# Loading two heads of keys and of values with one DMA in a cached-attention decode kernel

## The chip, the cores and the metric

The kernel runs on one core of one Trainium2 chip (trn2). The metric is device time in microseconds (us) of one execution. A trace shows one of these executions; its span, from the first to the last recorded work of the core, is about 2 us shorter than the time.

## The reference

One token passes through attention over the last 4096 positions of a key and value cache with 32 heads of 128 (64 MiB in bfloat16), and through a small gated MLP whose output multiplies the attention's.

```python
# W = 4096, 32 heads, Dh = 128, D = 512
q = (xn @ wq) per head
scores = q . k[:, last W positions] * Dh**-0.5
o = softmax(scores) @ v[:, last W positions]
s = o.reshape(1, 1, 32 * 128) @ wo
g = silu(B(xn))            # layer norms, w1..w4, gelu; at S = 1 its shifted terms are zero
out = x + s * g
```

## The kernel before

Every load goes through one queue, issued by the SyncE engine (SP) in program order, and the transfers finish in that order. One load brings one head: 128 partitions, 8 KiB in each (32 consecutive positions), 1 MiB.

```python
G = 4;  LAG = 5;  K_BUFS = 12;  V_BUFS = 7

def load(dst, src):
    return tc.keep_in_program_order(nc.sync.dma_start(out=dst, in_=src))
...
def load_kv(pool, cache, h):
    t = pool.tile([P, NC, Dh], BF16, tag="kv", name="kv")
    load(t[:], cache[0, h, W0:, :].rearrange("(p c) d -> p c d", p=P))
    return t
```

Even key heads go to VectorE (a product with the broadcast query, `prod`, then a sum, `sS`). Odd key heads go to TensorE: 32 transposes into `pt`, copied by ScalarE to `kt`, then 32 products `sT`. After four heads (a group) the softmax is formed on VectorE and TensorE. Values follow five heads behind the keys: 32 products per head into `oT`, then `o`. Heads are projected with `wo` in blocks of eight after a `repack` of `o`; the last heads with single rows of `wo` (`wo_rows`, `wo_few`).

```python
for i in range(H + LAG):
    if i < H:
        k_head(i, load_kv(k_pool, A_k_cache, i))
    ...
    if i >= LAG:
        h = i - LAG
        if h == H - 1:
            load_rows(h_part, H - G - h_part)      # wo rows of heads 26, 27
        v = load_kv(v_pool, A_v_cache, h)
        if h in (7, 15, 23):
            load_wo((h + 1) // 8 - 1)              # takes a buffer of the key ring
        ...
        if h == H - 1:
            load_rows(H - G, G - 1)
            load_rows(H - 1, 1)
        v_head(h, v)
```

The order within each engine is chosen when the program is built, not only by this text: a different set of loads can give a different order.

Of the kernel before, what the change touches and what calls it, by code (L numbers as in the profile page):

```python
# [8 lines left out]
P = 128  # L9
BF16 = mybir.dt.bfloat16  # L10
# [7 lines left out]

G = 4
LAG = 5  # L20
K_BUFS = 12
NE = 4
V_BUFS = 7


@with_exitstack
def kernel(
# [14 lines left out]
    nc = tc.nc  # L42

    Bb, Sq, D = A_x.shape
    assert Bb == 1 and Sq == 1, "decode kernel: B == Sq == 1"
    _, H, Sk, Dh = A_k_cache.shape
# [3 lines left out]
    W0 = Sk - W  # L50
    assert W == 4096
    NC = W // P
# [6 lines left out]

    k_pool = ctx.enter_context(tc.tile_pool(name="k", bufs=K_BUFS))  # L60
    kt_pool = ctx.enter_context(tc.tile_pool(name="kt", bufs=2))
# [13 lines left out]
    def load(dst, src):  # L75
        return tc.keep_in_program_order(nc.sync.dma_start(out=dst, in_=src))  # L76
# [14 lines left out]
    wq_sb = wts.tile([P, KC, HD], BF16, name="wq_sb")  # L91
    load(wq_sb[:], A_wq.rearrange("(p c) n -> p c n", p=P))

    def load_kv(pool, cache, h):
        t = pool.tile([P, NC, Dh], BF16, tag="kv", name="kv")
        load(t[:], cache[0, h, W0:, :].rearrange("(p c) d -> p c d", p=P))
        return t

    ident_bf = const.tile([P, P], BF16, name="ident_bf")
# [143 lines left out]
    for c in range(2):  # L243
        nc.vector.tensor_copy(
            out=few[:, c, 0:4 * NE].rearrange("p (a b) -> p a b", b=4),
# [14 lines left out]
    def flush():  # L260
        while pending:
            qk(*pending.pop(0))

    def k_head(h, kn):
        g, hl = divmod(h, G)
        if hl == 0:
            st[g] = {
                "sT": ps_s.tile([P, G // 2, NC], FP32, tag="sT", name="sT"),
                "sS": sm_pool.tile([P, G // 2, NC], FP32, tag="sS", name="sS"),
            }  # L270
        s = st[g]
        if h % 2 == 0:
            prod = prod_pool.tile([P, NC, Dh], BF16, tag="prod", name="prod")
            nc.vector.tensor_tensor(out=prod[:], in0=kn[:],  # L274
                                    in1=q_bc[:, h // 2:h // 2 + 1, :].to_broadcast([P, NC, Dh]),
                                    op=ALU.mult)
            nc.vector.tensor_reduce(out=s["sS"][:, hl // 2, :], in_=prod[:], axis=AX.X, op=ALU.add)  # L277
        else:
            kt = kt_pool.tile([P, NC, P], BF16, tag="kt", name="kt")
            for b in range(NB):  # L280
                pt = ps_tr.tile([P, 8, P], BF16, tag="pt", name="pt")
                for i in range(8):
                    nc.tensor.transpose(pt[:, i, :], kn[:, b * 8 + i, :], ident_bf[:])  # L283
                nc.scalar.copy(out=kt[:, b * 8:(b + 1) * 8, :], in_=pt[:])  # L284
                if b == 0:
                    flush()
            pending.append((s["sT"], hl, h, kt))
            if hl == G - 1:
                flush()
        if hl == G - 1:  # L290
            softmax(g)

    def softmax(g):
        s = st[g]
        m1 = sm_pool.tile([P, 2, G // 2], FP32, tag="m1", name="m1")
        nc.vector.tensor_reduce(out=m1[:, 0, :], in_=s["sS"][:], axis=AX.X, op=ALU.max)
        nc.vector.tensor_reduce(out=m1[:, 1, :], in_=s["sT"][:], axis=AX.X, op=ALU.max)  # L297

        mt_ps = ps_misc.tile([G, P], FP32, tag="misc", name="mt_ps")
        nc.tensor.transpose(mt_ps[:], m1[:].rearrange("p a b -> p (a b)"), ident_f[:])  # L300
        mx = sm_pool.tile([G, 1], FP32, tag="mx", name="mx")
        nc.vector.tensor_reduce(out=mx[:], in_=mt_ps[:], axis=AX.X, op=ALU.max)
        md = sm_pool.tile([G, G], FP32, tag="md", name="md")
        nc.vector.tensor_scalar(out=md[:], in0=ident_f[0:G, 0:G], scalar1=mx[:], scalar2=None,  # L304
                                op0=ALU.mult)
        mb_ps = ps_misc.tile([P, 2, G // 2], FP32, tag="misc", name="mb_ps")
        nc.tensor.matmul(mb_ps[:], lhsT=ones_f[0:G, :], rhs=md[:], start=True, stop=True)  # L307
        mb = sm_pool.tile([P, 2, G // 2], FP32, tag="mb", name="mb")
        nc.vector.tensor_copy(out=mb[:], in_=mb_ps[:])  # L309
        e = sm_pool.tile([P, 2, G // 2, NC], FP32, tag="e", name="e")  # L310
        for i, src in enumerate((s["sS"], s["sT"])):
            nc.vector.tensor_tensor(out=e[:, i], in0=src[:],  # L312
                                    in1=mb[:, i, :].unsqueeze(2).to_broadcast([P, G // 2, NC]),
                                    op=ALU.subtract)
        pT = sm_pool.tile([P, 2, G // 2, NC], BF16, tag="pT", name="pT")
        nc.scalar.activation(out=pT[:], in_=e[:], func=ACT.Exp, scale=scale)  # L316
        s["pT"] = pT
# [17 lines left out]
    o_blk, wo_blk = {}, {}  # L335

    def load_wo(i):
        t = k_pool.tile([P, 8, D], BF16, tag="kv", name="wo_8")
        wo_blk[i] = t
        load(t[:], A_wo[8 * i * P:8 * (i + 1) * P, :].rearrange("(p t) n -> p t n", p=P))  # L340

    def load_few():
        t = wo_blk[few_block]
        for c in range(2):
            r0 = 8 * few_block * P + c * FEW // 2
            load(t[32 * c:32 * c + 4 * NE],
                 A_wo[r0:r0 + FEW // 2, :].rearrange("(b a t) n -> a b (t n)", b=4, a=NE))
# [4 lines left out]
    def load_rows(h, n):  # L352
        load(wo_rows[:, h - h_part:h - h_part + n, :],
             A_wo[h * P:(h + n) * P, :].rearrange("(h p) n -> p h n", p=P))
# [33 lines left out]
    def v_head(h, v):  # L388
        g, hl = divmod(h, G)
        s = st[g]  # L390
        i = h // 8
        if hl == 0:
            softmax_den(g)
            s["oT"] = ps_o.tile([P, G], FP32, tag="oT", name="oT")
        if h % 8 == 0:
            o_blk[i] = sm_pool.tile([P, 8], BF16, tag="o", name="o")
            if i == few_block:
                nc.vector.memset(o_blk[i][:], 0.0)
        k = 2 * (hl % 2) + hl // 2
        oT, o = s["oT"], o_blk[i]  # L400
        for c in range(NC):
            nc.tensor.matmul(oT[:, k:k + 1], lhsT=v[:, c, :], rhs=s["pT"][:, hl % 2, hl // 2, c:c + 1],  # L402
                             start=(c == 0), stop=(c == NC - 1))
        if h >= H - G:
            nc.vector.tensor_tensor(out=o[:, h % 8:h % 8 + 1], in0=oT[:, k:k + 1],
                                    in1=s["rden"][:, k:k + 1], op=ALU.mult)
        elif hl == G - 1:

            nc.vector.tensor_tensor(  # L409
                out=o[:, h % 8 - 3:h % 8 + 1].rearrange("p (a b) -> p b a", b=2),  # L410
                in0=oT[:].rearrange("p (b a) -> p b a", b=2),
                in1=s["rden"][:].rearrange("p (b a) -> p b a", b=2), op=ALU.mult)
        ready, later[:] = later[:], []
        for f in ready:
            f()
        if h in (7, 15, 23, H - G - 1):
            def step(i=i):
                ox = repack(i)
                later.append(lambda: apply_wo(i, ox))
            later.append(step)  # L420


    v_pool = None
    for i in range(H + LAG):
        if i < H:
            k_head(i, load_kv(k_pool, A_k_cache, i))
        if i == LAG:
            wts_guard.__exit__(None, None, None)
            v_pool = ctx.enter_context(tc.tile_pool(name="v", bufs=V_BUFS))
            wo_blk[few_block] = v_pool.tile([64, 8, D], BF16, tag="wo_few", bufs=1, name="wo_few")  # L430
            nc.gpsimd.memset(wo_blk[few_block][:], 0.0)
            wo_rows = v_pool.tile([P, H - h_part, D], BF16, tag="wo_rows", bufs=1, name="wo_rows")
        if i >= LAG:
            h = i - LAG
            if h == H - 1:
                load_rows(h_part, H - G - h_part)
            v = load_kv(v_pool, A_v_cache, h)
            if h in (7, 15, 23):
                load_wo((h + 1) // 8 - 1)
            if h == H - 3 * G:  # L440
                load_few()
# [4 lines that stand above are left out]
# [38 lines left out]
```

## Time and profile before

| | before |
|---|---|
| median time | 197.74 us (3 runs, 197.67 to 197.79) |
| span of the profiled execution | 195.5 us |
| DMA, 20 to 185 us | share 1.01, 424 GB/s |
| busy: TensorE, VectorE, ScalarE | 64%, 66%, 35% |

The DMA rows of the page come first, because they are full while no compute engine is; the prediction shows them. Two lines of the list of DMA issues complete the picture (columns: tile and source, queue, count, size of one, median us from issue to landing).

```profile
kv<-in_A_k_cache_dram SPq DMA_DIRECT2D x32, 1024.0 KB, 19.6
kv<-in_A_v_cache_dram SPq DMA_DIRECT2D x32, 1024.0 KB, 19.6
```

There are 64 such loads, and the median one is under way for 19.6 us, because seven others stand before it.

### The profile page before, as it was taken

How to read it: one execution, taken by the hardware profiler on the slowest of the kernel's cores; microseconds unless marked ns; L12 is line 12 of the kernel's file. 1: busy time of each engine (PE TensorE's matmuls, PEld its weight loads, DVE VectorE, ACT ScalarE, POOL GpSimd, SP SyncE). 2: the span in 40 equal slices, each digit the busy share in tenths (PEclk: the TensorE clock that was granted, in tenths of full speed). 3: DMA queues.
4: the chain of work that ended last, by engine and by line, in shares of the span. 5: the costliest groups of instructions: out<-in, count | busy, mean ns of one | idle time of the engine just before them, and what ended most of it. 6: DMA issues, size and time to landing. Idle time of an engine off the chain costs nothing.

```text
span 195.5 us, 5353 instructions
## 1 busy us (share of the span) xinstructions
PE 125.0 (64%) x2448; PEld 113.4 (58%) x2448; DVE 129.6 (66%) x165; ACT 69.3 (35%) x82; POOL 5.8 (3%) x12
## 2 busy tenths in 40 slices
PE   0564496827969693099783772399584950798663
PEld 0463346827959683099683662299484950687552
DVE  1530059998979988985199919694699559691501
ACT  2003038709345270055453250077170610257000
POOL 2110007000000000000000000000000000000000
PEclk9999999675585555555558585576555555588555
DMA  6999899999999999999999999999999999999970
GB/s 209 409 496 426 372 424 419 424 426 417 426 424 426 426 424 422 422 427 427 422 424 427 422 424 422 427 426 422 422 427 424 424 422 427 429 424 417 418 292 8
DMA packets 11518, 79.18 MB, mean 405 GB/s; under 512 B 1384, under 2 KB 2248, under 8 KB 2504
## 3 DMA queue, kind: packets, MB, share of 16 engines
q1 hardware_dynamic: 11344, 78.85, 96.4%
q8 instruction: 19, 0.31, 0.6%
q10 hardware_dynamic: 152, 0.00, 0.0%
q14 instruction: 3, 0.02, 0.0%
HBM read 78.84 MB, written 0.00 MB: 403 GB/s over the span
## 4 chain that ended last, share of the span: by engine, by line
DMA 57%; PE 18%; DVE 16%; issue 3%; ACT 3%; SPq 1%; DVEq 0%; ACTq 0%
DMA kv<-in_A_v_cache_dram 30%; DMA kv<-in_A_k_cache_dram 18%; DMA wq_sb<-in_A_wq_dram 10%; DVE sS L277 7%; PE pt L283 7%; DVE prod L274 6%; PE oT L402 4%; PE sT L255 2%; ACT kt L284 2%; SPq L76 1%; PE mb_ps L307 1%; PE qT_ps L225 1%; PE qb_ps L234 1%; PE y_ps L139 1%; PE mt_ps L300 1%
## 5 line engine op out<-in xcount | busy, mean ns | idle before, releaser
L284 ACT COPY kt<-pt 128x1024 bf16<-128x1024 bf16 x64 | 60.2, 1026 | 68.2 <-PE pt L283 68.2
L277 DVE TENSOR_REDUCE sS<-prod 128x32 f32<-128x4096 bf16 x16 | 70.6, 4414 | 0.3
L283 PE MATMUL pt<-ident_bf,kv 128*128 128x128 bf16 x512 | 53.4, 298 | 3.4 <-DMA kv<-in_A_k_cache_dram 3.2
L283 PEld LDWEIGHTS <-kv 128*128 128x128 bf16 x512 | 49.8, 141 | 4.7 <-DMA kv<-in_A_k_cache_dram 3.4
L274 DVE TENSOR_TENSOR prod<-kv,q_bc 128x4096 bf16<-128x4096 bf16 x16 | 36.6, 2285 | 6.3 <-DMA kv<-in_A_k_cache_dram 4.1
L402 PEld LDWEIGHTS <-kv 128*128 128x128 bf16 x1024 | 30.6, 102 | 16.5 <-issue 10.0
L402 PE MATMUL oT<-pT,kv 128*128 128x1 bf16 x1024 | 32.6, 165 | 8.3 <-DVE o L409 4.2
L255 PE MATMUL sT<-qT_bf,kt 128*128 128x1 bf16 x512 | 20.4, 166 | 3.5 <-ACT kt L284 3.1
L255 PEld LDWEIGHTS <-kt 128*128 128x128 bf16 x512 | 18.2, 103 | 4.5 <-ACT kt L284 4.2
L297 DVE TENSOR_REDUCE m<-sT 128x2 f32<-128x64 f32 x8 | 1.8, 224 | 19.3 <-PE sT L255 19.3
L139 PEld LDWEIGHTS <-ox 128*1 128x1 bf16 x96 | 2.2, 114 | 19.5 <-DVE ox L369 19.5
L363 PE MATMUL ox_ps<-spread,to 128*128 128x64 bf16 x4 | 0.8, 212 | 17.4 <-DVE spread L360 17.4
L316 ACT ACTIVATE pT<-e 128x128 bf16<-128x128 f32 x8 | 2.5, 310 | 20.7 <-DVE e L312 20.7
L307 PEld LDWEIGHTS mb_ps<-md,ones_f 4*128 4x128 f32 x16 | 3.8, 290 | 6.1 <-DVE md L304 6.1
L307 PE MATMUL mb_ps<-md,ones_f 4*128 4x4 f32 x16 | 4.5, 347 | 4.4 <-DVE md L304 4.4
L322 PE MATMUL den_ps<-pT,ones_bf 128*128 128x128 bf16 x8 | 2.1, 265 | 7.3 <-ACT pT L316 7.2
L300 PE MATMUL mt_ps<-ident_f,m 128*4 128x128 f32 x8 | 2.7, 334 | 5.9 <-DVE m L297 5.9
L236 ACT CAST q_bc<-qb_ps 128x512 bf16<-128x512 f32 x4 | 2.3, 586 | 9.9 <-PE qb_ps L234 9.9
L234 PE MATMUL qb_ps<-wq_sb,xn_rep 128*128 128x512 bf16 x16 | 5.3, 506 | 0.0
L225 PE MATMUL qT_ps<-xn_bf,wq_sb 128*128 128x1 bf16 x64 | 1.9, 165 | 5.2 <-DMA wq_sb<-in_A_wq_dram 5.2
L225 PEld LDWEIGHTS <-wq_sb 128*128 128x128 bf16 x64 | 1.8, 104 | 5.5 <-DMA wq_sb<-in_A_wq_dram 5.5
L309 DVE COPY mb<-mb_ps 128x4 f32<-128x4 f32 x8 | 1.3, 163 | 5.3 <-PE mb_ps L307 5.3
(96 smaller groups left out, 61.6 us busy)
## 6 DMA issues: line engine op xcount, KB each, us to landing
kv<-in_A_k_cache_dram SPq DMA_DIRECT2D x32, 1024.0 KB, 19.6
kv<-in_A_v_cache_dram SPq DMA_DIRECT2D x32, 1024.0 KB, 19.6
wq_sb<-in_A_wq_dram SPq DMA_DIRECT2D x1, 4096.0 KB, 18.9
wo<-in_A_wo_dram SPq DMA_DIRECT2D x3, 1024.0 KB, 20.4
w_sb<-in_B_w_dram SPq DMA_DIRECT2D x1, 1376.0 KB, 6.7
w_sb<-in_B_w_dram SPq DMA_DIRECT2D x1, 1024.0 KB, 8.7
w_sb<-in_B_w_dram SPq DMA_DIRECT2D x1, 512.0 KB
wo_rows<-in_A_wo_dram SPq DMA_DIRECT2D x1, 384.0 KB, 17.5
```

The lines of the kernel that those rows point to most:

```text
L139: nc.tensor.matmul(ps[32 * j:32 * j + 1, :], lhsT=col, rhs=w[0:k, j * P:(j + 1) * P], start=False, stop=last, skip_group_check=True)
L225: nc.tensor.matmul(qT_ps[:, h:h + 1], lhsT=wq_sb[:, c, h * Dh:(h + 1) * Dh], rhs=xn_bf[:, c:c + 1], start=(c == 0), stop=(c == KC - 1))
L234: nc.tensor.matmul(qb_ps[:], lhsT=xn_rep[:, c, :], rhs=wq_h[:, c, 2 * i:2 * i + 8:2, :], start=(c == 0), stop=(c == KC - 1))
L255: nc.tensor.matmul(sT[:, hl // 2, c:c + 1], lhsT=kt[:, c, :], rhs=qT_bf[:, h:h + 1], start=True, stop=True)
L274: nc.vector.tensor_tensor(out=prod[:], in0=kn[:], in1=q_bc[:, h // 2:h // 2 + 1, :].to_broadcast([P, NC, Dh]), op=ALU.mult)
L277: nc.vector.tensor_reduce(out=s["sS"][:, hl // 2, :], in_=prod[:], axis=AX.X, op=ALU.add)
L283: nc.tensor.transpose(pt[:, i, :], kn[:, b * 8 + i, :], ident_bf[:])
L284: nc.scalar.copy(out=kt[:, b * 8:(b + 1) * 8, :], in_=pt[:])
L300: nc.tensor.transpose(mt_ps[:], m1[:].rearrange("p a b -> p (a b)"), ident_f[:])
L307: nc.tensor.matmul(mb_ps[:], lhsT=ones_f[0:G, :], rhs=md[:], start=True, stop=True)
L316: nc.scalar.activation(out=pT[:], in_=e[:], func=ACT.Exp, scale=scale)
L402: nc.tensor.matmul(oT[:, k:k + 1], lhsT=v[:, c, :], rhs=s["pT"][:, hl % 2, hl // 2, c:c + 1], start=(c == 0), stop=(c == NC - 1))
```

## The change

The intent is fewer and larger transfers: 2 MiB for two heads, with rings of 6 key pairs and 3 value pairs in about the same memory. The last two value heads stay single, so that the end still waits for a small transfer. The output weights get a buffer of their own.

```diff
-K_BUFS = 12
+K_BUFS = 6
-V_BUFS = 7
+V_BUFS = 3
...
-    def load_kv(pool, cache, h):
-        t = pool.tile([P, NC, Dh], BF16, tag="kv", name="kv")
-        load(t[:], cache[0, h, W0:, :].rearrange("(p c) d -> p c d", p=P))
+    pair = {}
+    def load_kv(pool, cache, h, split):
+        if h % 2 == 0:
+            t = pool.tile([P, 2, NC, Dh], BF16, tag="kv", name="kv")
+            pair[pool] = t
+            if h < split:
+                load(t[:].rearrange("p h c d -> p h (c d)"),
+                     cache[0, h:h + 2, W0:, :].rearrange("h (p c) d -> p h (c d)", p=P))
+        t = pair[pool][:, h % 2]
+        if h >= split:
+            load(t, cache[0, h, W0:, :].rearrange("(p c) d -> p c d", p=P))
         return t
...
-        t = k_pool.tile([P, 8, D], BF16, tag="kv", name="wo_8")
+        t = v_pool.tile([P, 8, D], BF16, tag="wo_8", bufs=1, name="wo_8")
...
-            k_head(i, load_kv(k_pool, A_k_cache, i))
+            k_head(i, load_kv(k_pool, A_k_cache, i, H))
...
-            v = load_kv(v_pool, A_v_cache, h)
+            v = load_kv(v_pool, A_v_cache, h, H - 2)
```

More of the change, by code (lines that the diff above doesn't have):

```diff
@@ L273, in k_head @@
             prod = prod_pool.tile([P, NC, Dh], BF16, tag="prod", name="prod")
-            nc.vector.tensor_tensor(out=prod[:], in0=kn[:],
+            nc.vector.tensor_tensor(out=prod[:], in0=kn,
                                     in1=q_bc[:, h // 2:h // 2 + 1, :].to_broadcast([P, NC, Dh]),
```

## The prediction

> **What bounds the kernel now.** I read the page's DMA rows first, then the stretches of 20 us, the waits of the DMA queue, the issues in order of time, and last VectorE and TensorE near the end.
>
> ```profile
> DMA  6999899999999999999999999999999999999970
> GB/s 209 409 496 426 372 424 419 424 426 417 426 424 426 426 424 422 422 427 427 422 424 427 422 424 422 427 426 422 422 427 424 424 422 427 429 424 417 418 292 8
> q1 hardware_dynamic: 11344, 78.85, 96.4%
> ...
> DMA 57%; PE 18%; DVE 16%; issue 3%; ACT 3%; SPq 1%; DVEq 0%; ACTq 0%
> ```
>
> The 16 DMA engines are full from the second slice to the last but two, at 417 to 429 GB/s once the weights are in. All 78.85 MB pass one queue; 78.85 MB at 425 GB/s is 185.5 us of a 195.5 us span. The rest is about 2.5 us before the first full microsecond and the tail after the last bytes.
>
> ```profile
> 60.00:80.00 20.00, 13.32 (x261) 12.83 (x259) 18.18 (x17) 7.83 (x9) 0.00 (x0) 0.50 1.01 424
> 120.00:140.00 20.00, 12.80 (x260) 11.84 (x260) 13.42 (x17) 7.52 (x8) 0.00 (x0) 0.59 1.01 425
> ```
>
> Columns: PE, PEld, DVE, ACT, POOL busy, granted clock, DMA share, GB/s. VectorE is nearly full only while it works off its late start; later it has about a third to spare, and the DMA share stays 1.01 in both. So compute can only matter if it fails to free a buffer in time, or after the last bytes.
>
> ```profile
> SPq L76 <- DMA kv<-in_A_v_cache_dram: 56.7, 27, 3.5
> SPq L76 <- DMA kv<-in_A_k_cache_dram: 56.4, 29, 2.1
> ...
> SPq L76 <- PE oT L402: 1.8, 3, 1.4
> ```
>
> The issuing queue waits for earlier transfers to land, hardly ever for a consumer: V buffers cost it 1.8 us in all. A K or V transfer lands 19.6 us (median) after its issue, eight times the 2.46 us between issues: eight transfers are always queued, and one leaves as one enters. That period is (96.22 - 59.34) / 15 = 2.459 us per MiB, or 426 GB/s, from:
>
> ```profile
> 59.34 0.33 SPq L76 DMA_DIRECT2D kv<-in_A_k_cache_dram  x1
> ...
> 96.22 0.33 SPq L76 DMA_DIRECT2D kv<-in_A_v_cache_dram  x1
> ...
> 173.04 0.33 SPq L76 DMA_DIRECT2D kv<-in_A_v_cache_dram  x1
> ```
>
> The last line is value head 31, which waited 1.4 us for a buffer, yet landed in step with the full queue.
>
> **What the Trainium skill says.** "HBM Reference", section Specifications: one core streaming alone gets about 425 GB/s, bounded by its DMA engines. The trace agrees (424 to 426). "DMA: Bandwidth & Descriptors", section Where 436 GB/s comes from: the ceiling is 435.2 GB/s. That leaves at most 2.459 - 1.0486/0.4352 = 2.459 - 2.409 = 0.05 us per MiB for everything that a transfer and its packets add. The same page, section Measured, has 341 GB/s for 1 MB and 425 for 16 MB, and advises larger transfers. The trace disagrees for this queue: with eight waiting, 1 MiB transfers already run at 426, so that gain is not to be had again. Its section Latency and other measured facts warns of row pitches of large powers of two (8 MiB between partitions: 103 GB/s). The two heads of a pair are 32768 x 128 x 2 B = 8 MiB apart, but the 128 partitions stay 8 KiB apart; no run here shows whether two alternating addresses matter.
>
> **The change part by part.**
>
> Transfers: K goes from 32 to 16, V from 32 to 15 + 2 = 17, so 31 fewer; bytes and contiguous rows (8 KiB) are unchanged. If all of the 0.05 us were per transfer, 31 x 0.05 = 1.55 us would go; but 8 data packets per engine stay, so I take half: -0.8 us. This lies on the path, since the queue is full. Issue time (0.33 us each) lies beside it.
>
> Memory: 12 + 7 buffers of 8 KiB become 6 + 3 pairs of 16 KiB and one of 8 KiB for the output weights, 152 KiB both ways. The V ring holds 6 heads instead of 7, and is freed by two heads at a time.
>
> Start: head 0 landed near 24.9 us, and VectorE began on it at 26.62, held by the query cast (2.17 us of wait). The pair lands 2.46 us later, 27.3: VectorE starts 0.7 us later, inside a backlog that it works off by 83.92. The queue holds keys until 37 us, V is let in when the weights' memory comes free at 29.4 as now. Nothing for the end.
>
> Does the V ring starve the queue? In transfer time a K pair and a V pair take 9.84 us. V heads 6 and 7 need heads 0 and 1 consumed: TensorE finished these at 51.2, with the later start 51.9. Ahead of them then are queued K and V up to key 11, whose landing I count as 66.6 (37.1 + 6 x 4.92). Their bytes must begin at about 65: some 11 us spare with 2 us for getting under way. Heads 10 and 11 need 4 and 5 (consumed at 67.5, so 68.3) and begin near 87: 17 us spare. The tightest is at the end: head 30 opens a new pair and needs 24 and 25 consumed. Today that is
>
> ```profile
> 172.07 0.94 PE L402 MATMUL oT<-pT,kv 128*128 128x1 bf16 x32
> ...
> 173.91 0.97 PE L402 MATMUL oT<-pT,kv 128*128 128x1 bf16 x32
> ```
>
> at 174.9; its bytes begin near 182.5. With up to 2 us delay from the next part, 3 to 4 us remain. So no gap.
>
> VectorE and the end: odd keys go to TensorE, even ones to VectorE. In the stream an odd key keeps its place, but its even partner now lands with it, 4.9 us later than now. Today:
>
> ```profile
> 147.13 2.29 DVE L274 TENSOR_TENSOR prod<-kv,q_bc 128x4096 bf16<-128x4096 bf16 x1 [0.19 <-DMA kv<-in_A_k_cache_dram]
> 149.45 4.42 DVE L277 TENSOR_REDUCE sS<-prod 128x32 f32<-128x4096 bf16 x1
> ...
> 157.34 0.23 DVE L297 TENSOR_REDUCE m<-sT 128x2 f32<-128x64 f32 x1 [3.21 <-PE sT L255]
> ...
> 166.50 0.15 DVE L409 TENSOR_TENSOR o<-oT,rden 128x4 bf16<-128x4 f32 x1
> ...
> 169.19 2.29 DVE L274 TENSOR_TENSOR prod<-kv,q_bc 128x4096 bf16<-128x4096 bf16 x1 [1.45 <-DMA kv<-in_A_k_cache_dram]
> ```
>
> Key 27 reached TensorE at 151.99; its pair lands there. VectorE then runs 2.29 + 4.42 = 6.8 us and the maximum follows at about 159.1 instead of 157.34: +1.75 us. Its 3.2 us of slack per group is eaten and replaced by its own work. Per group of four heads (19.7 us of transfers) VectorE needs 2 x 6.7 + 2.5 for the softmax + 1 = 17 us, so it still keeps pace.
>
> For the last group keys 30 and 31 land near 174.1: scores end 180.85, maximum at 181.1 against 180.05 today, +1.0 us. TensorE at the end:
>
> ```profile
> 187.97 0.99 PE L402 MATMUL oT<-pT,kv 128*128 128x1 bf16 x32 [0.25 <-DVE o L405]
> ...
> 190.58 1.01 PE L402 MATMUL oT<-pT,kv 128*128 128x1 bf16 x32 [1.31 <-DMA kv<-in_A_v_cache_dram]
> ```
>
> It waited 1.31 us for head 31. A chain later by 1.0 fits in that; if the repacking before key 29 holds TensorE back as today (its wait for VectorE moves from 166.5 to about 168.6, and key 31 with it), the chain is 2.1 us late and 0.8 us shows. I take half: +0.4 us. The last values stay single, so the order and size of the last transfers, and the last wait, are as now.
>
> Sum: 197.74 - 0.8 + 0.4 = 197.3 us.
>
> **The rivals.** One: larger transfers raise the rate to the ceiling. Speaks for it: fewer completions; against it: 0.05 us per MiB is all that is left. It would give 196.2 with no loss at the end; even removing the whole 0.05 us for about 75 MiB gives 194.0, just short of 2%. Two: a wait for consumers takes the place of the wait for landings, because a V pair frees only when both heads are done. For it: the V ring was touched already (1.8 us); against it: the 11 and 17 us above. Its place would be heads 28 to 31; if those are issued 2 to 4 us late, 199 to 201. Three: two rows 8 MiB apart slow the memory. Against it: the 16 engines' addresses still differ as now. At 1% less, 199.5; at 3%, 203. Four: the instruction order changes with the new loads and TensorE waits elsewhere, within 1 us either way.
>
> **Range and chances.** Parts one to four and the terms of the sum, each of about 1 us, give 195.9 to 198.9 for eight in ten. Faster by 2% means under 193.8, more than the whole overhead: 0.03. Slower by 2% means over 201.7, a starved queue or slower memory: 0.05. Within: 0.92.
>
> **What would show it.** Right: the DMA share stays at 1.01 and 424 to 428 GB/s from 40 to 185 us; pairs issue on freed V buffers, not on landings, so the queue's waits for TensorE grow without a gap in the GB/s row; landing times roughly double or more; VectorE's even keys wait for the pair's landing, and its wait for the odd key's scores goes to near zero. Wrong: any slice below 410 in the middle (starved or slower memory; the waits of the queue tell which), a mean above 430 (overhead larger than thought), or a final wait after the last value head that differs from the 5 us now by more than 1 us (a tail set by VectorE and TensorE).

## The result, and the profile after

| | before | after |
|---|---|---|
| median time, same chip | 197.77 us (6 runs, 197.67 to 198.76) | 198.50 us (6 runs, 198.34 to 198.62) |
| ratio | | 1.0028 (95%: 1.0008 to 1.0048) |
| span of the profiled execution | 195.5 us | 196.6 us |

A ratio is the mean time of one kernel's runs over the mean of the other's of the same rounds, so it is not quite the ratio of the medians. The change is within 2%, and a little slower; a second set of rounds (after_again below) gave 1.0034 (1.0022 to 1.0046).

First the page of the changed kernel: DMA rows, queue, chain and issues.

```profile
DMA  6999899999999999999999999999999999999950
GB/s 203 407 497 423 373 422 420 423 430 415 430 420 423 427 425 423 425 428 422 427 423 427 422 423 427 430 422 428 422 427 423 427 422 428 422 432 423 416 197 5
q1 hardware_dynamic: 10848, 78.84, 95.8%
...
DMA 58%; DVE 27%; PE 7%; SPq 2%; ACT 2%; issue 1%; DVEq 0%; ACTq 0%
...
kv<-in_A_k_cache_dram SPq DMA_DIRECT2D x16, 2048.0 KB, 29.7
kv<-in_A_v_cache_dram SPq DMA_DIRECT2D x15, 2048.0 KB, 27.9
```

No slice in the middle is below 415. The queue has 496 packets fewer (11344 - 10848): 31 transfers times 16 engines, that is, one small packet per engine and transfer. The stretch from 20 to 185 us, kernel before and then kernel after (the last two columns are the DMA share and GB/s):

```profile
20.00:185.00 165.00, 111.89 (x2164) 102.73 (x2165) 123.10 (x125) 66.16 (x77) 3.50 (x1) 0.62 1.01 424
```

```profile
20.00:185.00 165.00, 113.47 (x2131) 103.28 (x2131) 122.43 (x121) 66.19 (x77) 3.50 (x1) 0.64 1.01 424
```

The rate is the same to the last digit. Summing rate times length over the stretches of each trace gives the bytes that have arrived by a moment, in MB. This table is the shortest view of a kernel whose transfers never stop:

| by (us) | before | after |
|---|---|---|
| 20 | 7.52 | 7.52 |
| 100 | 41.34 | 41.30 |
| 180 | 75.33 | 75.34 |
| 190 | 79.10 | 79.07 |

Neither a gain nor a gap. The waits of the queue (after) show that the reason for waiting has changed all the same:

```profile
SPq L76 <- PE oT L412: 36.9, 10, 9.5
SPq L76 <- DMA kv<-in_A_v_cache_dram: 34.4, 10, 9.1
...
SPq L76 <- DMA kv<-in_A_k_cache_dram: 3.5, 2, 2.1
```

The queue now waits 36.9 us for TensorE to release a value pair, where it waited 1.8 us before. This long wait of the issuing queue cost nothing in the stream, because transfers issued earlier kept the engines full: the DMA share stayed at 1.01.

So the loss lies after the stream. VectorE and TensorE at the end, in order of time (start, us, engine and line, what; idle time before it in brackets):

```profile
174.23 2.29 DVE L284 TENSOR_TENSOR prod<-kv,q_bc 128x4096 bf16<-128x4096 bf16 x1 [4.26 <-DMA kv<-in_A_k_cache_dram]
176.55 4.42 DVE L287 TENSOR_REDUCE sS<-prod 128x32 f32<-128x4096 bf16 x1
...
181.02 0.21 DVE L306 TENSOR_REDUCE m<-sS 128x2 f32<-128x64 f32 x1
```

```profile
184.47 0.27 PE L332 MATMUL den_ps<-pT,ones_bf 128*128 128x128 bf16 x1 [1.06 <-ACT pT L326]
185.03 1.01 PE L412 MATMUL oT<-pT,kv 128*128 128x1 bf16 x32 [0.30 <-DMA kv<-in_A_v_cache_dram]
...
190.90 0.27 PE L149 MATMUL y_ps<-wo_rows,o 128*1 128x128 bf16 x1 [0.44 <-issue]
191.10 1.01 PE L412 MATMUL oT<-pT,kv 128*128 128x1 bf16 x32
```

Key 30 reaches VectorE at 174.23 (before: 169.19), and the maximum of its scores comes at 181.02. Value head 28 starts at 185.03 (before: 183.00), and waits for its transfer in doing so. Head 31 starts at 191.10 (before: 190.58), no longer after a wait for its transfer but right behind a pause of 0.44 us with no recorded wait. Last, the output transfer, before and after:

```profile
192.88 0.59 SPq L76 DMA_DIRECT2D out_dram<-out_row  x1
```

```profile
193.34 0.59 SPq L76 DMA_DIRECT2D out_dram<-out_row  x1
```

It is issued 0.46 us later. From the end of the issue to the end of the span it takes 195.5 - 193.47 = 2.03 us before and 196.6 - 193.93 = 2.67 us after: 0.64 us more, for the same 1 KB. The two parts make up the 1.1 us between these two spans.

### The profile page after: what moved, and what is told of

It reads as the page before. It is cut to its first block, busy times and chain, and to the rows that moved or that the text cites. A ratio compares the mean times of both kernels' runs of the same rounds, so it can differ in the third digit from the quotient of the medians.

```text
span 196.6 us, 5309 instructions
## 1 busy us (share of the span) xinstructions
PE 127.8 (65%) x2448; PEld 115.1 (59%) x2448; DVE 129.7 (66%) x165; ACT 69.3 (35%) x82; POOL 5.8 (3%) x12
## 3 DMA queue, kind: packets, MB, share of 16 engines
q1 hardware_dynamic: 10848, 78.84, 95.8%
## 4 chain that ended last, share of the span: by engine, by line
DMA 58%; DVE 27%; PE 7%; SPq 2%; ACT 2%; issue 1%; DVEq 0%; ACTq 0%
DMA kv<-in_A_k_cache_dram 43%; DVE sS L287 16%; DMA kv<-in_A_v_cache_dram 13%; DVE prod L284 8%; PE oT L412 4%; SPq L76 2%; DMA x_bf<-in_A_x_dram 2%; ACT kt L294 2%; PE y_ps L149 1%; PE mb_ps L317 1%; PE mt_ps L310 1%; DVE mx L312 1%; PE pt L293 0%; DVE e L322 0%; DVE md L314 0%
## 5 line engine op out<-in xcount | busy, mean ns | idle before, releaser
L293 PE MATMUL pt<-ident_bf,kv 128*128 128x128 bf16 x512 | 54.1, 298 | 17.2 <-DMA kv<-in_A_k_cache_dram 16.8
L412 PE MATMUL oT<-pT,kv 128*128 128x1 bf16 x1024 | 30.7, 165 | 4.0 <-DMA kv<-in_A_v_cache_dram 3.8
L244 PE MATMUL qb_ps<-wq_sb,xn_rep 128*128 128x512 bf16 x16 | 6.2, 573 | 0.0
L334 DVE TENSOR_REDUCE den<-den_ps 128x4 f32<-128x128 f32 x8 | 2.3, 292 | 5.6 <-PE den_ps L332 5.6
L312 DVE TENSOR_REDUCE mx<-mt_ps 4x1 f32<-4x128 f32 x8 | 2.2, 278 | 4.6 <-PE mt_ps L310 4.6
L154 PE MATMUL ln_ps<-x_f,ones_f 128*128 128x4 f32 x4 | 1.2, 364 | 5.6 <-DVE x_f L177 4.9
```

Of the source, the lines that this page charges most:

```text
L244: nc.tensor.matmul(qb_ps[:], lhsT=xn_rep[:, c, :], rhs=wq_h[:, c, 2 * i:2 * i + 8:2, :], start=(c == 0), stop=(c == KC - 1))
L293: nc.tensor.transpose(pt[:, i, :], kn[:, b * 8 + i, :], ident_bf[:])
L312: nc.vector.tensor_reduce(out=mx[:], in_=mt_ps[:], axis=AX.X, op=ALU.max)
L412: nc.tensor.matmul(oT[:, k:k + 1], lhsT=v[:, c, :], rhs=s["pT"][:, hl % 2, hl // 2, c:c + 1], start=(c == 0), stop=(c == NC - 1))
```

## The experiments

Twelve runs were made, all with correct results and five rounds. "Level" means that the interval of the ratio holds 1. The runs were made on four chips in groups, and the changed kernel itself ran again only in the first group (after_again); the others are compared with it through the kernel before on their own chip.

| run | median us | before, same chip | ratio (95%) |
|---|---|---|---|
| after_again | 198.43 | 197.74 | 1.0034 (1.0022 to 1.0046) |
| keys_tail_single | 199.29 | 197.74 | 1.0080 (1.0050 to 1.0109) |
| pairs_v_only | 198.07 | 197.74 | 1.0012 (0.9999 to 1.0025) |
| pairs_k_only | 197.66 | 197.74 | 0.9996 (0.9984 to 1.0008) |
| values_tail4_single | 198.31 | 197.87 | 1.0034 (1.0004 to 1.0065) |
| both_tails_single | 198.02 | 197.87 | 1.0028 (1.0000 to 1.0056) |
| fewer_matmuls | 198.14 | 197.87 | 1.0013 (0.9998 to 1.0027) |
| sp_padded | 198.28 | 197.86 | 1.0005 (0.9983 to 1.0028) |
| rings_only | 197.82 | 197.86 | 1.0013 (0.9980 to 1.0046) |
| rows_4k | 200.19 | 197.86 | 1.0110 (1.0090 to 1.0130) |
| rows_4k_two_dmas | 201.01 | 197.86 | 1.0157 (1.0134 to 1.0180) |
| both_tails_padded | 197.61 | 197.74 | 0.9986 (0.9967 to 1.0005) |

**A disturbance to know first.** Some executions of several kernels, the one before among them (198.7 to 199.8 us), are 1 to 2 us longer than their neighbours. Three profiles fell on such an execution (keys_tail_single, pairs_v_only, values_tail4_single). By 20 us they had moved 7.01, 7.11 and 7.08 MB instead of 7.52; the rates were normal afterwards, and the deficit stayed. Their ends are therefore about 1 us late (0.40 to 0.49 MB by 180 us at 424 GB/s), which I take off below. What held the transfers between 15 and 20 us I do not know. The ratios contain such runs on both sides, so I give the undisturbed times as well where it matters.

**1. The changed kernel again (after_again).** No edit.

> The changed kernel once more, as the control for the runs beside it. All theories: 1.002 to 1.004 of the kernel before (0.4 to 0.8 us slower), no slice of the GB/s row below 415 in the middle. Open: in its first profile TensorE stood still for 0.44 us at 190.46 with no recorded wait, and the span ran 2.7 us past the issue of the output transfer against 2.0 us in the kernel before. If these two are properties of the program they come again (0.3 to 0.6 us each); if they are chance, they are gone here.

Its time was 198.43 us. Both oddities came again: the pause (0.51 us, again in front of the last product with the head-27 rows) and the long end (196.6 us of span, output issued from 193.36 to 193.94, so 2.66 us). They are properties of the program.

**2. Last keys single (keys_tail_single).**

```diff
-k_head(i, load_kv(k_pool, A_k_cache, i, H))
+k_head(i, load_kv(k_pool, A_k_cache, i, H - 2))
```

> The changed kernel with its last two key heads (30, 31) loaded by two transfers of 1 MiB instead of one of 2 MiB. Theory A (the end is set by VectorE and TensorE, late because key 30 now lands with key 31): VectorE takes up key 30 4 to 5 us earlier, TensorE stops being the last to be ready and waits about 1 us for value head 31 again, and the kernel is 0.4 to 0.6 us faster than the changed one, level with the kernel before (0.999 to 1.001). Theory B (the end comes from the loads: the V ring or the landing of the last value): no change against the changed kernel, 1.002 to 1.004.

Not faster. Three runs took 199.90 to 200.44 us (the profiled one, with the late start, among them), the others 198.48 to 198.68, as the changed kernel. Theory A fell. The trace says why (its times are 1.2 us late):

```profile
185.96 1.01 PE L412 MATMUL oT<-pT,kv 128*128 128x1 bf16 x32 [1.52 <-DMA kv<-in_A_v_cache_dram]
```

The softmax was earlier, but TensorE then stood 1.52 us in front of value head 28, which now lands only with head 29. After correction it starts at 184.8, where the changed kernel has 185.03.

**3. Values only in pairs (pairs_v_only)** and **4. keys only in pairs (pairs_k_only).** The other kind has single loads and as many buffers as heads in the changed ring (12 or 6).

```diff
 # pairs_v_only                                  # pairs_k_only
-K_BUFS = 6                                      -V_BUFS = 3
+K_BUFS = 12                                     +V_BUFS = 6
+def load_one(pool, cache, h):  # the load of before, one head
-    k_head(i, load_kv(k_pool, A_k_cache, i, H))     # pairs_v_only
+    k_head(i, load_one(k_pool, A_k_cache, i))
-    v = load_kv(v_pool, A_v_cache, h, H - 2)        # pairs_k_only
+    v = load_one(v_pool, A_v_cache, h)
```

> Only values are loaded in pairs (ring of 3 pairs, last two single); keys are single in a ring of 12, the output weights have a buffer of their own. Theory A: keys land as before, so the end is as before: 0.999 to 1.001. Theory B (the V ring of 3 pairs costs the time): 1.002 to 1.004, as the full change. If transfers had a cost of their own, the 15 fewer of them would give up to 0.4 us: 0.998.

> Only keys are loaded in pairs (ring of 6 pairs); values are single in a ring of 6. Theory A: the whole loss is here, 1.002 to 1.004, with TensorE not waiting for value head 31 at the end. Theory B: no loss, 0.998 to 1.001.

Theory A had it the wrong way round: keys in pairs alone cost nothing, values in pairs alone cost about 0.3 us (five of six runs from 197.83 to 198.21). In the values-only trace TensorE waited 1.77 us for head 28, as in run 2. The keys-only trace has no such wait, and a maximum that is earlier, not later, than in the changed kernel, because single values put the last key pair before head 25 in the queue instead of behind it. So the two runs do not isolate one term each; a load's place in the order moves with the pairing of the other kind.

**5. Four values single (values_tail4_single)** and **6. both ends single (both_tails_single).**

```diff
-v = load_kv(v_pool, A_v_cache, h, H - 2)
+v = load_kv(v_pool, A_v_cache, h, H - 4)
 # both_tails_single has this and the edit of run 2
```

> The changed kernel with four value heads (28 to 31) loaded singly at the end instead of two. Theory C (after the last-keys run failed: TensorE's last stretch is held by two things that come ready at almost the same time, the softmax of the last group, late by the key pair, and value head 28, which now lands with head 29; taking away either alone leaves the other): head 28 lands 2.4 us earlier, near 182.6, but its weights of the softmax are still only ready at 184.7, so TensorE begins on it near 184.75 instead of 185.0: at most 0.3 us faster than the changed kernel, 1.0015 to 1.003 of the kernel before. If the value pair alone is the cause: 0.999 to 1.001.

> The changed kernel with the last two key heads and the last four value heads loaded singly. Theory C: both holds are gone, head 28 begins near 183 as in the kernel before, TensorE waits 1 us or more for head 31 at the end, and the time is level with the kernel before: 0.999 to 1.001 (leaving out runs with a start that is 1 us late, as three of the six of the last-keys run had). If something else holds the end (transfers, the V ring): 1.0025 to 1.004 as the changed kernel.

With the values alone (times 1.05 us late), head 28 waits for no transfer any more; it starts the moment the softmax lets it:

```profile
185.45 0.27 PE L332 MATMUL den_ps<-pT,ones_bf 128*128 128x128 bf16 x1 [1.06 <-ACT pT L326]
185.51 1.04 PE L412 MATMUL oT<-pT,kv 128*128 128x1 bf16 x32
```

That is 184.46 after correction, 0.57 us before the changed kernel; its undisturbed runs took 198.04 to 198.38. With both:

```profile
183.38 0.99 PE L412 MATMUL oT<-pT,kv 128*128 128x1 bf16 x32
...
190.47 1.01 PE L412 MATMUL oT<-pT,kv 128*128 128x1 bf16 x32 [0.78 <-DMA kv<-in_A_v_cache_dram]
```

Head 28 starts at 183.38, and TensorE waits for head 31 again, from 190.47 (before: 190.58). Theory C holds: two things come ready within 0.3 us of each other in the changed kernel, the softmax late by the key pair and head 28 late by the value pair, and removing one leaves the other. The output is issued at 192.81, even before that of the kernel before. The wait for head 31 was 0.78 us, where 1 us or more was expected. Yet the four undisturbed runs took 197.96 to 198.05, still some 0.2 us more than the 197.8 of the undisturbed runs of the kernel before on that chip, and the span still ends 2.6 us after the issue. The second term is elsewhere.

**7. Fewer early matmuls (fewer_matmuls).** The products dropped multiply a vector of zeros, so the result stays right.

```diff
-for c in range(KC):
-    nc.tensor.matmul(hs_ps[:, j:j + 1], lhsT=w2_sb[:, c, j::4],
-                     rhs=shifted_bf[:, c:c + 1], start=(c == 0), stop=(c == KC - 1))
+nc.tensor.matmul(hs_ps[:, j:j + 1], lhsT=w2_sb[:, 0, j::4],
+                 rhs=shifted_bf[:, 0:1], start=True, stop=True)
```

> The changed kernel without 12 of the 16 early products of a vector that is all zeros (the result stays right); it only moves every later TensorE instruction 12 weight loads and 12 matmuls forward in the program. In the changed kernel TensorE stands still 0.44 to 0.51 us just before the last product with the head-27 rows, in both of its profiles. If that is a refill of the instruction stream at a fixed place of the program, the pause moves 12 weight loads later, into the products of value head 31, and the time stays at 1.003. If it is a wait for data, it stays in front of the same instruction.

No pause shows in this trace, and the time was 198.14 us, 0.3 us under that of after_again (on another chip). Head 31 in its trace:

```profile
190.73 1.05 PE L411 MATMUL oT<-pT,kv 128*128 128x1 bf16 x32 [0.45 <-DMA kv<-in_A_v_cache_dram]
```

The product with the head-27 rows needs the same data as before, so the pause is no wait for data; it depends on where the instructions lie in the program. The traces show more than that, in their list of DMA packets (the page only counts them). The queue that the page calls "q8 instruction" moves 16 KB at a time. In all 14 traces TensorE's 2403rd weight load (the 2404th in pairs_v_only, whose program has one more) starts 2.26 to 2.53 us after such a packet starts. Where TensorE would have come to it sooner, the pause stands there; it is the last product of head 27 in both traces of the changed kernel. In fewer_matmuls the 2403rd load lies 12 loads further on, inside head 31, as foreseen, and TensorE comes to it 2.38 us after the packet, too late to have to wait. A refill of the instruction stream fits all 14; no run delays that packet alone, so it stays likely and not shown. The run also sizes the pause: with all its late softmax and late head 28, the changed kernel would have waited for head 31 until about 190.73; with the pause it begins at 191.10.

**8. A longer program for the issuing queue (sp_padded).** The rest of the loss came after the output's issue. I counted the instructions of each built program by engine: in the changed kernel only SyncE's has become much shorter, 85 against 133.

```diff
+    load(scratch[:, n, :], A_x[0, 0, :].rearrange("(p c) -> p c", p=16))  # 1 KB, read by nobody
 # behind each pair from head 10 on: 20 more instructions of this kind, with their waits 111 in all
```

> The changed kernel with 20 extra loads of 1 KB that nothing reads, one behind every pair from head 10 on. They only make the issuing queue's program longer again: 111 instructions against 85, where the kernel before has 133, keys-only pairs 119, values-only pairs 105. In every profile so far the span ends 2.0 to 2.1 us after the issue of the output transfer where that program has 105 or more, and 2.6 to 2.8 us where it has 85 to 87. If its length decides it, this run ends 2.0 to 2.1 us after the issue, with no 27 GB/s of traffic in the last 0.3 us, and is 0.3 to 0.6 us faster than the changed kernel (1.000 to 1.0015 of the kernel before; the loads themselves may cost up to 0.3 us). If it comes from the pairs in another way, the end stays at 2.6 us or more.

The long end is gone:

```profile
span 196.3 us, 5335 instructions
```

```profile
191.29 0.27 PE L155 MATMUL y_ps<-wo_rows,o 128*1 128x128 bf16 x1 [0.62 <-issue]
```

```profile
193.72 0.60 SPq L76 DMA_DIRECT2D out_dram<-out_row  x1
```

The span ends 2.0 us after the issue, as in every program of 105 to 133 such instructions (2.0 to 2.1), where programs of 85 to 87 have 2.6 to 2.8. The 8 KB or so that the changed kernel moves in its last 0.3 us (the last column is GB/s) are gone as well; in the changed kernel:

```profile
196.30:196.60 0.30, 0.00 (x0) 0.00 (x0) 0.00 (x0) 0.00 (x0) 0.00 (x0) 0.50 0.09 27
```

The time gained less than expected. The runs took 197.68 to 198.41 us in two clusters that I can't explain. The ratio of 1.0005 is flattered by two disturbed runs of the kernel before (198.81 and 198.84); without them it is 1.0015, the edge of the expected band, and the median is 0.15 us under that of after_again, where 0.3 to 0.6 us were expected. In the profiled run the output is issued 0.38 us later than in the changed kernel: head 28 begins 0.21 us later (185.24), and the pause before the last product of head 27 is 0.62 us here, 0.18 us more.

Run 8 adds transfers as well as instructions, so by itself it does not tell which of the two counts. The traces do. They hold the instructions of SyncE in the order of its program (two fewer than the built program has), and SyncE stands idle for about 0.45 us in front of the 80th of them, whatever that is:

| run | recorded instructions of SyncE | the 80th starts at (us) | idle before it (us) | end of the output's issue to end of span (us) |
|---|---|---|---|---|
| before | 131 | 125.13, a load | 0.45 | 2.03 |
| after | 83 | 195.79, behind the output | 0.46 | 2.67 |
| after_again | 83 | 195.81, behind the output | 0.46 | 2.66 |
| both_tails_single | 85 | 195.16, behind the output | 0.47 | 2.61 |
| sp_padded | 109 | 149.03, a load | 0.45 | 1.98 |

The same holds in keys_tail_single, values_tail4_single and fewer_matmuls (behind the output) and in pairs_k_only, rings_only, rows_4k and both_tails_padded (at a load); in pairs_v_only and rows_4k_two_dmas a wait overlaps it. In both_tails_single, with two loads more than the changed kernel, the idle time lies two instructions earlier in the end of the program. So the place in SyncE's program decides: in the long programs the 80th instruction is issued in the middle of the stream, where 0.45 us of SyncE cost nothing, and with 83 to 85 instructions it falls behind the output transfer. The 27 GB/s are one packet of 8 KB of the queue "q14 instruction", at 196.43 us; that queue's third packet comes at 128.31 us before and at 152.40 us in sp_padded.

**9. Rings alone (rings_only).** Single loads as before, but 6 value buffers and the output weights in their own.

```diff
-V_BUFS = 7
+V_BUFS = 6
-t = k_pool.tile([P, 8, D], BF16, tag="kv", name="wo_8")
+t = v_pool.tile([P, 8, D], BF16, tag="wo_8", bufs=1, name="wo_8")
```

> The kernel before with the memory of the change but none of its pairs: single loads, 6 value buffers instead of 7, output weights in a buffer of their own, 12 key buffers. If the smaller V ring alone cost anything, 1.001 to 1.003. I expect 0.999 to 1.001: no gap in the transfers, the end as in the kernel before.

Level: 197.82 against 197.86 us, two of six runs disturbed, the profiled span 195.5 us. The smaller ring of values and the buffer for the output weights are not a cause by themselves.

**10. 4 KiB rows (rows_4k)** and **11. the same in two transfers (rows_4k_two_dmas).** Both from the kernel before; they measure the cost that the prediction split in half without a measurement.

```diff
-load(t[:], cache[0, h, W0:, :].rearrange("(p c) d -> p c d", p=P))
+src = cache[0, h, W0:, :].rearrange("(b p c) d -> p b (c d)", b=2, p=P)
+load(t[:].rearrange("p (b c) d -> p b (c d)", b=2), src)             # rows_4k
+for b in range(2):                                                   # rows_4k_two_dmas
+    load(t[:].rearrange("p (b c) d -> p b (c d)", b=2)[:, b], src[:, b])
```

> The kernel before with a different assignment of positions to partitions (the same in keys and values, so the result is right): every load still one transfer of 1 MiB, but of 4 KiB rows, 16 packets per engine instead of 8. It measures the cost of a packet. If half of the 0.05 us per MiB that I took for overhead were per packet, 8 more packets per engine for 64 loads would cost 64 x 0.025 = 1.6 us: 1.008. If packets of this size cost nothing: 0.999 to 1.002.

> As the run with 4 KiB rows, but each load cut into two transfers of 512 KiB: the same packets, 64 more transfers. It doubles the suspected cost per transfer, against the 4 KiB run of the same call. With the 0.025 us per transfer of the prediction it would be 1.6 us slower than that run (0.8%); the changed kernel's cumulative bytes say about zero, so I expect within 0.2% of it, with half the data in flight (eight transfers of 512 KiB) still enough to keep the engines full.

The stretch from 25 to 180 us of the kernel before, of rows_4k and of rows_4k_two_dmas:

```profile
25.00:180.00 155.00, 106.11 (x2030) 97.95 (x2028) 120.43 (x112) 65.85 (x76) 3.50 (x1) 0.60 1.01 424
```

```profile
25.00:180.00 155.00, 102.69 (x1963) 92.87 (x1962) 120.42 (x112) 63.97 (x75) 3.50 (x1) 0.66 1.02 418
```

```profile
25.00:180.00 155.00, 104.08 (x1964) 94.90 (x1962) 122.11 (x112) 64.01 (x75) 3.50 (x1) 0.62 1.03 417
```

Bytes that arrived between 25 and 180 us: 65.75 MB before, 65.82 changed, 64.77 with 4 KiB rows, 64.70 with 4 KiB rows and twice the transfers. In time per MiB (155 us x 1.0486 MB / bytes) that is 2.472, 2.469, 2.509 and 2.512 us. Eight more packets per engine and MiB, each half as long, cost 0.037 us, 4.7 ns each; the kernel's 1.0110 is more than the 1.008 that half of the overhead would have given. (The run does not tell the number of packets from the shorter rows that they read.) One more transfer per MiB costs 0.003 us, which is about the reading's error. The second run was 0.8 us slower than the first, against an expected 0.4 us at most, but not by its stream: its output is issued 0.28 us later (195.62 against 195.34), with a different order on TensorE, and its span ends 2.9 us after the issue's end against 2.1. This long end is another one than that of run 8: SyncE (195 recorded instructions) does not stand idle there, but waits 1.79 us for the output to land, where the kernel before waits 0.89 us. One packet of "q14 instruction" (8 KB) starts at 196.81 us, just ahead of the output's own packets; whether it holds them up was not tested.

**12. Both causes removed, the pairs kept (both_tails_padded).** The edits of runs 6 and 8 together.

> The closing test: pairs everywhere but in the last two key heads and the last four value heads, and the issuing queue's program made longer by the same extra loads of 1 KB as in the padded run. Both causes found for the loss are taken away, the pairs stay. If they are all of it: TensorE waits for head 31 again (its products begin near 190.5 to 190.8), the span ends 2.0 to 2.1 us after the issue of the output transfer, and the time is level with the kernel before, 0.999 to 1.002 among runs without a late start. If more was lost in the pairs themselves: above 1.002.

```profile
190.78 1.01 PE L418 MATMUL oT<-pT,kv 128*128 128x1 bf16 x32 [0.80 <-DMA kv<-in_A_v_cache_dram]
...
193.02 0.60 SPq L76 DMA_DIRECT2D out_dram<-out_row  x1
```

TensorE waits for head 31, the span (195.6 us) ends 2.0 us after the issue, and the time is 197.61 us: level with the kernel before. With both causes removed, the remaining pairs are neither a gain nor a loss. No run beats the kernel before by more than its interval.

## Why the prediction was right or wrong

The time, 198.5 us, lies in the range and in the class "within 2%", but on the other side of the kernel before: the forecast was -0.4 us, and +0.7 us was measured. Point by point:

- **The bound: right.** The queue stayed full, and the starving rival was rightly refused: TensorE's releases became the queue's main wait (36.9 us) and the stream had no gap. Landing times rose to 28 to 30 us; the forecast "roughly double or more" was too high.
- **Transfers, -0.8 us: wrong, about zero.** The failing step is "8 data packets per engine stay, so I take half". Of the 0.05 us of overhead per MiB, 8 x 4.7 ns = 0.037 us belong to the packets by an estimate from run 10, and the packets stayed. Per transfer run 11 found 0.003 us, and the changed kernel's stream 2.469 us per MiB against 2.472. The first rival (larger transfers) falls with it, and so does the third: transfers with rows 8 MiB apart ran at the same 424 GB/s.
- **VectorE late by the key pair: right in mechanism and size.** The maxima were forecast at about 159.1 and 181.1 and came at 158.99 and 181.02; the wait for the odd key's scores went to zero. (A slip of the sum, 2.29 + 4.42 = 6.8 instead of 6.7, does not matter here.)
- **The end, +0.4 us: right in size (0.46 us at the output's issue), but partly by luck, since the cause was incomplete.** The step "The last values stay single, so the order and size of the last transfers, and the last wait, are as now" overlooked that head 28 lands with head 29 and that TensorE's last stretch hangs on it: the repacking of the block before, which the program places after head 28, as much as heads 29 to 31. With both late, TensorE's slack of 1.31 us was gone, so that a pause without a recorded wait came into the open. Runs 2, 5 and 6 show the two holds; run 7 shows that the pause depends on the place in the program, and sizes it at about 0.4 us.
- **The end of the program, +0.6 us: not foreseen by any rival.** Removing 31 transfers shortened SyncE's program, and the span ended 0.64 us later after the output. The prediction's only step on issuing, "Issue time (0.33 us each) lies beside it", did not ask what the removal of 31 issues moves. Of the 0.64 us, 0.46 us are SyncE's idle time before its 80th instruction, which the shorter program moves behind the output; that instruction itself then takes 0.11 us, where the same one took 0.01 us before. Run 8 moves the idle time back into the stream by lengthening the program, and its place is the same in every trace where no wait overlaps it. That it is a fetch of instructions is likely, not shown.

The terms thus read: 0 for the transfers, about +0.5 us before the output and +0.6 us behind it in the profiled pair. Over all runs the median times differ by 0.7 us and the mean spans by 0.9 us (196.5 against 195.6), so these terms vary a little from run to run. The two errors (0.8 us of gain that did not come, 0.6 us of loss not foreseen) point the same way, so the forecast had the wrong sign, and the time stayed in the range because that was about 1.5 us wide on either side.

## What to carry to other kernels

Where a queue already kept the DMA engines full with eight transfers of 1 MiB waiting, merging transfers gained nothing, while halving the packets' size cost 1.5% of the rate; packets above 8 KiB were not tried. A table of bytes arrived against time settles it in one look. Merging makes the first half of each transfer as late as the second, so follow every consumer near the end, not only the last one, and expect two holds side by side: test them alone and together. Differences of half a microsecond can come from where instructions lie in an engine's program; look at the time between the output's issue and the end of the span before explaining them by the data, and compare at which instruction of its program an engine stands idle, not only at what time.

## What the Trainium skill lacked or had wrong

- "DMA: Bandwidth & Descriptors", section Why small descriptors are slow, gives a fixed cost of about 3 cycles per packet; at the 850 MHz that the page has for the fabric that is an estimate of 3.5 ns. These runs agree roughly, with 4.7 ns, but the cost still shows at 4 KiB against 8 KiB rows (1.5% of the rate), and what the page leaves open is that one transfer more per MiB costs hardly anything beside it once others are queued (0.003 us, within the reading).
- "Runtime: NRT & Kernel Launch", section Instruction fetch mechanics, says that crossing a 16 KiB block of instructions is mostly hidden. It gives no size for when it is not. Here SyncE stood idle for 0.45 to 0.47 us at its 80th recorded instruction in every trace where no wait overlapped it, which lengthened the end of the program (2.67 against 2.03 us) where it fell there, and TensorE paused 0.44 to 0.73 us before its 2403rd weight load when it came there sooner than about 2.3 us after a 16 KB instruction packet; that these are fetches is likely, not shown.
- No page has the disturbance of the start: in some executions 0.4 to 0.5 MB less arrived between 15 and 20 us, about 1 us that is never made up.
